# Fused attention and sine MLP: another opening order, the seven-product chain one block later, two of its products swapped

## The chip, the cores and the metric

The kernel runs on one core of a Trainium2 chip. The metric is the device time of one execution in microseconds (us), the median of several runs. The five engines named below are PE (TensorE, matrix products), ACT (ScalarE, table functions and copies), DVE (VectorE, element-wise work), POOL (GpSimd) and SP (SyncE, which here only starts DMAs).

## The reference

Eight batches of eight heads, 576 positions, head size 64. Attention adds a bias that depends on the distance of two positions; its output is reshaped to 4608 tokens of 512 features and goes through a two-layer MLP with a "snake" activation:

```
scores = q @ k.T / 8 + bias_table[bucket(|i - j|)]
attn   = softmax(scores)            # rows of 576
x      = (attn @ v)  as  (4608, 512)
h      = x @ w_in                   # w_in  512 x 2048
g      = h + sin(alpha*h)**2 / (alpha + 1e-9)
out    = g @ w_out                  # w_out 2048 x 512
```

## The kernel before

**Stages.** There is one stage for each batch t = 0..7. A stage has an exp phase and a sin phase, since ACT holds one function table at a time: `tbl` swaps it. In the exp phase PE forms the scores of a head pair and 128 keys (`plan_unit`; kind "A", and small kinds "B", "C" and "X" for the last 64 positions), ACT takes their exponential into `u` (L719), DVE multiplies the band near the diagonal by a table `m2r` or `mhr` of exponentials of the bias (L750, L736), PE multiplies by `v` with a column of ones (`plan_av`), DVE divides by the row sums (L964, L965), and the result is transposed into `xT`, by PE (L1036) and a copy or by a DMA. In the sin phase `plan_moe_in` takes a block b of 512 tokens: for each of 16 slices f of the hidden layer four matmuls `xT,w_in`, then `s` = sin (ACT, L1080), `sq` = s*s (ACT or DVE), and `g` (DVE, L1094). The last stage does two blocks.

**The output product.** Block b is multiplied by `w_out` in stage b+1, wherever PE has room. `plan_mo` does it row by row: four rows of 128 tokens, each 16 matmuls of 512 columns, `w_out,g`. For rows 2 and 3 of the blocks 1 to 6 `plan_chain` takes its place. It is a scheme with seven products in place of eight: two rows by two halves of the hidden layer by two halves of the output columns. Each product is 8 matmuls of 256 columns. DVE makes sums of `g` first (`pre`, into `ss` and into `g`), and the products need four differences of quarters of `w_out`, `wsum`, which `plan_wsum` computes once in stage 1. `take(k, ...)` is what empties product k out of PSUM: a copy to `zz`, or a DVE addition into `outs` (L1367). Two products share a PSUM bank, 0 with 1, 2 with 3, 4 with 5, and 6 has one alone; before, product 4 is `sums(0)` by `wsum[0]` and is emptied twice (`w` and `c22`), and product 5 is `act(1,1)` by `wsum[3]`.

**The order of the work.** Nothing is scheduled at run time. A planner in the kernel (`Plan.run`) places every task on its engine with assumed durations, priorities `pri` and earliest times `nb`, and the program is emitted in that order; on the chip each engine runs its own list in order and waits on semaphores. `QUOTA` and `QUOTA1` bound how many matmuls of the output product may go between the scores of an exp phase (`QUOTA1` for stage 1). `pad` puts filler matmuls on `zz` behind a task of the opening, and `Plan.fill` puts fillers where the planner sees PE idle.

**The opening (stage 0).** The first q and k come as they lie in memory. `plan_tr` transposes a head pair on PE (L562 for the first pair, L568) and a copy puts it into `kT` or `qT` (DVE L551; ACT L549 takes some for batch 1). The tables `m2r` and `mhr` go through DRAM and come back with DMAs on SP's queue. POOL issues `w_in` behind a copy (`tick`, L645) that waits for the last part of `m2r`, and behind `w_in`, on the same queue, the q and k of batch 1 (`nat2`), the four parts of `w_out` (slices f = 0-3, 4-7, 8-11, 12-15) and v of batch 1.

Of the kernel before, what the change touches and what calls it, by code (L numbers as in the profile page):

```python
# [211 lines left out]
WINDOW = 700  # L212
WARM_END = 22.0
QUOTA = 44
QUOTA1 = 32
OFFSET = 0
T_START = 4.0
STEPS = {0: ((1, 1, 1, 1),) * 3, 1: ((3, 1),) * 3}
# [4 lines left out]
T_CL = 24.5  # L223
T_FIRST = (4.75, 5.95)
T_PAIR = ((7.9, 8.5), (9.3, 10.2), (11.6, 12.3))
T_ACT = ()
T_M2 = (13.0, 14.8, 16.0, 16.0)
T_MH = 14.2
T_RST = 25.0
T_V0 = (5.8, 6.4, 8.9, 9.6)  # L230
T_P3 = 7.0
# [7 lines left out]
T_LD = 33.0  # L239

MIX = "nnssss"
CH = ("mo", "mo", "mo", "st")
PIECES = 4
AV_LATE = 9000
# [32 lines left out]
def kernel(  # L277
# [275 lines left out]
    def plan_tr(t, p, kq, pri, nb, deps=()):  # L553

        b, c = Buf("mo"), Cell()

        def mm(e):
            c.v = bank(b).bitcast(F16)
            for i in range(SI):
                x = i * SN  # L560
                if t == 0 and p == 0:
                    nc.tensor.transpose(  # L562
                        out=c.v[:, x : x + SN], in_=natb[:, kq, i], identity=id_sb[0:SN, 0:SN]
                    )
                    continue
                for z in range(2):
                    h = 2 * p - 2 + z if t == 0 else 2 * p + z
                    nc.tensor.transpose(  # L568
                        out=c.v[64 * z : 64 * z + 64, x : x + SN],
                        in_=(nat1 if t == 0 else nat2)[:, kq, h, D * i : D * i + D],  # L570
                        identity=id_sb[0:SN, 0:SN],
                    )

        def cp(e):
            pin = c.v[:, 0:S].rearrange("d (i p) -> d p i", i=SI)

            dst = (kTs, qTs)[kq][t][:, p, :]
            copy_on(e, dst.rearrange("d (p i) -> d p i", i=SI), pin)

        m = plan.add({"PE": 0.4 if t == 0 and p == 0 else 0.5}, mm, deps, pri, nb, new=[b])  # L580
        if t == 0:
            m.pad = (256,) if p else (192,) * (2, 3)[kq]
        eng = {"DVE": 0.75, "ACT": 0.6}
        if t == 0:
            eng = {"ACT": 0.65} if p in T_ACT and kq else {"DVE": 0.75}
        x = plan.add(eng, cp, [m], pri, use=[b])
        if kq:
            return [x], [x]

        def tail(e):  # L590
            for z in range(2):
                r = slice(64 * z, 64 * z + 64)
                k_of(e).tensor_copy(
                    out=kts[t][r, p, r], in_=kTs[t][r, p, 512:S]
                )

        return [x], [plan.add({"POOL": 0.4 if t == 0 else 0.5}, tail, [x], pri + 30)]
# [179 lines left out]
    def plan_att0(g, gates, gate):  # L777

        u, ub, done = Cell(), Buf("u"), {}
        a, b = 2 * g, 2 * g + 1  # L780
        runs = ((a, "A", 0), (a, "A", 1), (a, "A", 2), (a, "C", 0), (a, "A", 3),
                (b, "A", 0), (b, "A", 1), (b, "C", 0), (b, "A", 2), (b, "A", 3))
        exps, head = [], []
        for i, unit in enumerate(runs):
            base = PB + 3200 * g + 300 * i
            x = plan_unit(0, *unit, u, ub, done, gate, base)
            p, kind, _ = unit
            deps = gates + tr[(0, p, 0)][1 if kind == "C" else 0] + tr[(0, p, 1)][0]

            def run(e, i=i, x=x):  # L790
                if i == 0:
                    if g == 0:
                        plan.in_qk, plan.used = True, 0
                        plan.quota = QUOTA
                    u.v = new_u()
                plan.share = (g * len(runs) + i + 1) / (2 * len(runs))
                if g == 1 and i == len(runs) - 1:
                    plan.in_qk = False
                x[2](e)

            d, ends = run_time([unit + (False,)])
            m = plan.add({"PE": d}, run, deps, base, after=head,
                         new=([ub] if i == 0 else []) + [x[0]], use=[] if i == 0 else [ub])
            m.pad = (256,)
            m.offs = ([0.0] if i == 0 else []) + [0.1]
            m.marks = [(x[1], ends[0])]
            head = [m]
            exps += [x[3]]
        for p in (a, b):
            for w in range(2):  # L810
                base = PB + 3200 * g + 600 * ((2, 4)[w] if p == a else 4) + 50 * w
                plan_av(0, [(p, 256 * w), (p, 256 * w + 128)], u, ub, done, base, False)
        return exps
# [66 lines left out]
    def plan_late(base, gate):  # L880

        tb, done = tails[0] = Buf("ut"), {}
        units = [(0, "B", 0), (2, "B", 0), (0, "X", 0)]
        made = [plan_unit(0, *x, None, tb, done, gate, base + 30 * k) for k, x in enumerate(units)]

        def run(e):
            for x in made:
                x[2](e)

        m = plan.add({"PE": 0.78}, run, pe_gate, base, new=[tb] + [x[0] for x in made])  # L890
        m.offs = [0.0, 0.1, 0.32, 0.6]
        m.marks = [(x[1], o) for x, o in zip(made, (0.32, 0.54, 0.78))]
        tail_alone(0, base + 1200)
        return [x[3] for x in made]
# [75 lines left out]
    def plan_av(t, parts, u, ub, done, base, dma):  # L970

        nq = len(parts)
        ab, xb, tb = Buf("av"), Buf("xn"), Buf("h")
        av, xn, tr_ = Cell(), Cell(), Cell()
        prev = []
        p0, q0 = parts[0]
# [187 lines left out]
    def plan_wsum(t, deps):  # L1164
# [9 lines left out]
        )  # L1174
        k, x, y = todo[t]
        for i, d in enumerate(deps):
            r = slice(2 * i, 2 * i + 2)

            def sm(e, k=k, x=x, y=y, r=r):
                nc.vector.tensor_tensor(out=wsum[:, k, r], in0=x[:, r], in1=y[:, r], op=ALU.subtract)  # L1180

            wdone.append(plan.add({"DVE": 0.36}, sm, [d] + wdone[-4:], PB + 9500))

    wdone = []

# [102 lines left out]
    def plan_chain(b, a):  # L1288
# [92 lines left out]
        p = prod(1, lambda: act(0, 1), wq(1, 0), [])  # L1381
        c11 = take(1, (0, 0), (2, 0), [p, x], True)
        yield
        p = prod(2, lambda: sums(1), ws(1), [s2, x] + wdone)
        y = take(2, (1, 1), (2, 0), [p, x], True)
        p = prod(3, lambda: act(1, 0), ws(2), [s3])
        v = take(3, (1, 0), (1, 1), [p, y])
        yield
        p = prod(4, lambda: sums(0), ws(0), [])
        w = take(4, (0, 1), (1, 1), [p, y])  # L1390
        c22 = take(4, (1, 1), (1, 0), [p, v, w])
        p = prod(5, lambda: act(1, 1), ws(3), [])
        take(5, (1, 0), (1, 0), [p, v, c22], last=True)
        yield
        p = prod(6, lambda: sums(2), wq(1, 1), [s4])
        take(6, (0, 1), (0, 1), [p, w, c11], last=True)
# [16 lines left out]
    for t in range(T):  # L1413
# [4 lines left out]
        exps = []  # L1418
        for p in range(NP - 1) if t == 0 else ():
            for kq in range(2):  # L1420
                tr[(0, p + 1, kq)] = plan_tr(0, p + 1, kq, (150, 650, 5)[p], T_PAIR[p][kq])
        if t == 0:
            for g in range(2):
                exps += plan_att0(g, pe_gate, gate)
        else:
            exps += plan_att(t, pe_gate, gate)
            if t == 1:
                for i in range(4):
                    plan_wsum(i, exps[3 * i + 1 : 3 * i + 4] + exps[3 * i + 3 : 3 * i + 4])
            if t == 1:  # L1430
                exps += plan_late(PB + LATE, gate)
        if t == 0:
# [21 lines left out]
            sins += s_  # L1454
        pe_gate = [m]
        if t < T - 1:
            if t:
                rows, ch = iter((0, 1)), plan_chain(t, 2)
                for x in MIX:
                    if x == "n":  # L1460
# [3 lines left out]
            else:  # L1464
                for a in range(4):
                    plan_mo(t, a)
        else:
            for b in (t, t + 1):
                for a in (0, 2):
# [32 lines left out]
```

## Time and profile before

| what | value |
|---|---|
| median of 3 runs | 369.23 us (368.93 to 372.27) |
| the profiled execution, its own time | 368.74 us |
| its span (first to last instruction) | 366.8 us, so 1.9 us lie around it |
| granted TensorE clock | 1.0 |
| PE busy | 356.8 us, 97% of the span |
| ACT busy | 312.3 us, 85% |
| DVE busy | 309.2 us, 84% |
| POOL busy | 92.0 us, 25% |

All times in rows are us from the span's start. A row of the timeline has the start, the length, the engine, the line, the operation, its names and shapes, how many instructions were merged, and in brackets the idle time ahead of it with what ended that. Matmuls overlap: a row of n matmuls lasts n-1 intervals and the length of one. So a "busy" PE can still have lost some tenths of a microsecond at a gap, since the next matmul needs its full length again before its result is there.

### The profile page before, as it was taken

What the parts mean: (1) busy time and instruction counts of PE and PEld (TensorE: products, weight loads), DVE (VectorE), ACT (ScalarE), POOL (GpSimd) and SP (SyncE); (2) the same over time, 40 slices, a digit from 0 to 9 for tenths busy, and PEclk for the clock granted to TensorE, in tenths of its full rate; (3) what the DMA queues carried; (4) which work ended last, traced back from release to release, by engine and by line L of the source; (5) the groups of instructions that cost most, each with busy time, mean ns of one, the idle gap of its engine ahead of it and who ended that gap; (6) DMA issues with size and microseconds to landing.
All of it is one profiled execution on the core that took longest, in us unless ns stands there. A gap on an engine that the chain in (4) does not pass through costs nothing.

```text
span 366.8 us, 9604 instructions
## 1 busy us (share of the span) xinstructions
PE 356.8 (97%) x3808; PEld 218.9 (60%) x3808; DVE 309.2 (84%) x748; ACT 312.3 (85%) x430; POOL 92.0 (25%) x133
## 2 busy tenths in 40 slices
PE   7889999999999999999999999999999999999996
PEld 3464545644475446885684457545776468456685
DVE  4797979878977998699978998798869997899982
ACT  3988999889897999799988999799979997996711
POOL 7477350064000830047000900082006000000000
PEclk9999999999999999999999999999999999999999
DMA  9999999599724996299917992599529421001122
GB/s 170 198 172 204 200 162 148 115 97 122 111 53 102 127 150 108 78 143 113 152 52 153 87 173 55 134 125 128 104 79 163 35 79 50 15 2 57 44 74 87
DMA packets 150269, 40.53 MB, mean 110 GB/s; under 512 B 137208, under 2 KB 145616, under 8 KB 150224
## 3 DMA queue, kind: packets, MB, share of 16 engines
q0 software_dynamic: 96032, 17.67, 59.6%
q1 hardware_dynamic: 54016, 22.16, 25.9%
q8 instruction: 30, 0.49, 0.6%
q14 instruction: 15, 0.12, 0.1%
q10 hardware_dynamic: 176, 0.09, 0.1%
HBM read 37.73 MB, written 16.56 MB: 148 GB/s over the span
## 4 chain that ended last, share of the span: by engine, by line
PE 83%; ACT 10%; DVE 4%; issue 2%; ACTq 0%
PE pb L469 82%; ACT u L719 8%; ACT s L1080 1%; DVE outs L1367 1%; DVE u L750 1%; ACT sq L1087 1%; PE pb L1036 1%; PE pb L568 0%; ACT kT L549 0%; DVE nat L763 0%; ACT qT L549 0%; DVE xn L965 0%; PE pb L562 0%; DVE qT L551 0%; DVE zz L551 0%
## 5 line engine op out<-in xcount | busy, mean ns | idle before, releaser
L719 ACT ACTIVATE u<-pb 128x1024 f16<-128x1024 f32 (+1 forms) x146 | 136.8, 1022 | 10.3 <-PE pb L469 9.6
L469 PE MATMUL pb<-xT,w_in 128*128 128x512 f16 (+4 forms) x704 | 128.1, 340 | 0.0
L1094 DVE SCALAR_TENSOR_TENSOR g<-sq,inv_a,pb 128x512 f16<-128x512 f16 x144 | 101.1, 743 | 3.7 <-ACT sq L1087 2.0
L1080 ACT ACTIVATE s<-pb,alphaT 128x512 f16<-128x512 f32 x144 | 92.8, 693 | 12.8 <-PE pb L469 12.0
L469 PEld LDWEIGHTS <-w_in 128*128 128x128 f16 x704 | 64.7, 98 | 56.1 <-issue 0.3
L469 PE MATMUL pb<-w_out,g 128*128 128x512 f16 (+1 forms) x416 | 81.7, 339 | 0.5 <-DVE zz L551 0.5
L469 PEld LDWEIGHTS <-g 128*128 128x128 f16 x552 | 51.4, 98 | 37.6 <-issue 7.2
L750 DVE TENSOR_TENSOR u<-u,m2r 128x512 f16<-128x512 f16 (+1 forms) x128 | 61.6, 489 | 11.4 <-ACT u L719 8.6
L469 PEld LDWEIGHTS <-u 128*128 128x128 f16 x1280 | 56.0, 97 | 9.1 <-issue 3.8
L414 POOL COPY kt<-kT 64x256 f16<-64x256 f16 x12 | 5.2, 432 | 172.4 <-DMA kT<-staged_k 142.9
L1087 ACT ACTIVATE sq<-s 128x512 f16<-128x512 f16 x69 | 43.4, 639 | 2.0 <-DVE g L1094 1.1
L469 PE MATMUL pb<-qT,kT 64*128 64x64 f16 (+1 forms) x512 | 42.7, 285 | 1.8 <-DVE qT L551 0.6
L469 PE MATMUL pb<-v,u 128*128 128x65 f16 x1024 | 44.1, 193 | 0.3 <-DVE u L750 0.2
L1089 DVE TENSOR_TENSOR sq<-s 128x512 f16<-128x512 f16 x75 | 31.7, 432 | 10.8 <-ACT s L1080 10.1
L965 DVE TENSOR_TENSOR xn<-pb,rd 128x256 f16<-128x256 f32 (+2 forms) x59 | 28.5, 483 | 2.0
L469 PEld LDWEIGHTS <-kT 64*128 64x128 f16 x512 | 16.1, 94 | 22.4 <-issue 15.4
L469 PE MATMUL pb<-vh,u 128*128 128x130 f16 x128 | 28.2, 221 | 0.1
L419 POOL DMA_DIRECT2D v<-in_v_dram x28 | 24.8, 896 | 3.9 <-DMA nat<-in_k_dram 2.3
L1403 ACT ACT_TABLE_LOAD x15 | 19.2, 1283 | 0.3
L469 PE MATMUL pb<-wsum,g 128*128 128x256 f16 (+1 forms) x136 | 18.6, 266 | 0.9
L719 ACT ACTIVATE nat<-pb 128x1024 f16<-128x1024 f32 (+1 forms) x24 | 17.7, 817 | 0.0
L1367 DVE TENSOR_TENSOR outs<-pb,outs 128x256 f32<-128x256 f32 x30 | 12.6, 421 | 5.3 <-PE pb L469 4.7
(97 smaller groups left out, 303.0 us busy)
## 6 DMA issues: line engine op xcount, KB each, us to landing
out_dram<-outs SPq DMA_DIRECT2D x28, 256.0 KB, 2.9
v<-in_v_dram POOLq DMA_DIRECT2D x28, 128.0 KB, 4.5
staged_k<-in_k_dram POOLq DMA_DIRECT2D x6, 576.0 KB, 8.6
staged_q<-in_q_dram POOLq DMA_DIRECT2D x6, 576.0 KB, 12.4
w_in<-in_moe_w_in_dram POOLq DMA_DIRECT2D x4, 512.0 KB, 8.4
w_out<-in_moe_w_out_dram POOLq DMA_DIRECT2D x4, 512.0 KB, 14.7
out_dram<-outs SPq DMA_DIRECT2D x15, 128.0 KB, 1.7
w_out<-in_v_dram SPq DMA_DIRECT2D x6, 128.0 KB, 4.3
```

The source lines that it names most:

```text
L414: nc.gpsimd.tensor_copy(out=kts[t % 2][r, :, r], in_=kTs[t % 2][r, :, 512:S])
L419: nc.gpsimd.dma_start(out=vs[t % 2][:, c, :, 0:D], in_=vp[128 * c : 128 * c + 128],)
L469: nc.tensor.matmul(out=out, lhsT=lhsT, rhs=rhs, start=start, stop=stop, skip_group_check=go_on)
L719: nc.scalar.activation(out=o, in_=x, func=AF.Exp, scale=0.125)
L750: nc.vector.tensor_tensor(out=io, in0=io, in1=m2[:, 2 * p : 2 * p + 2, x0 : x0 + hi - lo], op=ALU.mult)
L965: nc.vector.tensor_tensor(out=xn[:, 0:n].rearrange("p c (z d) -> p c z d", z=2), in0=x[:, :, :, 0:D], in1=r.unsqueeze(3).to_broadcast([128 ...
L1080: nc.scalar.activation(out=s16.v, in_=h.v, func=AF.Sin, scale=alphaT[:, f : f + 1])
L1087: nc.scalar.activation(out=sq.v, in_=s16.v, func=AF.Square)
L1089: k_of(e).tensor_tensor(out=sq.v, in0=s16.v, in1=s16.v, op=ALU.mult)
L1094: nc.vector.scalar_tensor_tensor(out=gcell[b].v[:, f, :], in0=sq.v, scalar=inv_a[:, f : f + 1], in1=h.v, op0=ALU.mult, op1=ALU.add,)
L1367: nc.vector.tensor_tensor(out=put(i, j), in0=at(k), in1=put(*x), op=ALU.add)
L1403: nc.scalar.preload_act_table_set(name)
```

## The change

- **The chain one block later** (`FIRST = 2`): block 1 has all four rows by `plan_mo`. What chain 1 issued for the staging of batch 3 (POOL DMAs `staged_k`, `staged_q`) is planned in stage 1.
- **`wsum`**: two of the four differences in stage 1 and two in stage 2, in 32 pieces of 256 elements a row in place of 16 of 512.
- **Products 4 and 5 of the chain change places**: `act(1,1)` by `wsum[3]` is first, in the first half of the bank, and `sums(0)` by `wsum[0]`, emptied twice, is second. Product 2 no longer lists the copy of product 0 as a dependency.
- **`QUOTA1`** 44 in place of 32.
- **The opening**: no `pad` behind the transposes of pairs 1 to 3 nor behind the scores; other priorities and earliest times for the transposes (`T_TP`) and the bands (`T_M2`, `T_MH`); the last pair's `attn @ v` may take any bank (`P_ST`).
- Two assumed durations of the planner (`plan_tr`'s copy on ACT, the late scores of batch 0).

In the built program PE has 16 fillers of 256 columns fewer and 5 of 192 more; 32 more matmuls `w_out,g` of 512 columns, and 56 fewer of 256 columns. DVE has 750 instructions before and 742 after, ACT 436 and 438, POOL and SP as many as before.

```diff
-QUOTA1 = 32
+QUOTA1 = 44
...
 T_PAIR = ((7.9, 8.5), (9.3, 10.2), (11.6, 12.3))
+T_TP = ((450, 450), (650, 650), (5, 5))
 T_ACT = ()
-T_M2 = (13.0, 14.8, 16.0, 16.0)
-T_MH = 14.2
+P_ST = 3
+T_M2 = (14.85, 15.9, 17.0, 17.0)
+T_MH = 15.9
...
 MIX = "nnssss"
+SUMS = {1: (0, 1), 2: (2, 3)}
+FIRST = 2
...
         if t == 0:
-            m.pad = (256,) if p else (192,) * (2, 3)[kq]
-        eng = {"DVE": 0.75, "ACT": 0.6}
+            m.pad = () if p else (192,) * (2, 3)[kq]
+        eng = {"DVE": 0.75, "ACT": 0.53}
...
-            m.pad = (256,)
             m.offs = ([0.0] if i == 0 else []) + [0.1]
...
-        m = plan.add({"PE": 0.78}, run, pe_gate, base, new=[tb] + [x[0] for x in made])
+        m = plan.add({"PE": 0.5}, run, pe_gate, base, new=[tb] + [x[0] for x in made])
...
-        ab, xb, tb = Buf("av"), Buf("xn"), Buf("h")
+        ab, xb, tb = Buf("st" if t == 0 and parts[0][0] >= P_ST else "av"), Buf("xn"), Buf("h")
...
-            r = slice(2 * i, 2 * i + 2)
+            r = slice(i, i + 1)
...
-            wdone.append(plan.add({"DVE": 0.36}, sm, [d] + wdone[-4:], PB + 9500))
+            wdone.append(plan.add({"DVE": 0.218}, sm, [d] + wdone[-8:], PB + 9500))
...
-        p = prod(2, lambda: sums(1), ws(1), [s2, x] + wdone)
+        p = prod(2, lambda: sums(1), ws(1), [s2] + wdone)
...
-        p = prod(4, lambda: sums(0), ws(0), [])
-        w = take(4, (0, 1), (1, 1), [p, y])
-        c22 = take(4, (1, 1), (1, 0), [p, v, w])
-        p = prod(5, lambda: act(1, 1), ws(3), [])
-        take(5, (1, 0), (1, 0), [p, v, c22], last=True)
+        prod(4, lambda: act(1, 1), ws(3), [])
+        p = prod(5, lambda: sums(0), ws(0), [])
+        w = take(5, (0, 1), (1, 1), [p, y])
+        c22 = take(5, (1, 1), (1, 0), [p, v, w])
+        take(4, (1, 0), (1, 0), [p, v, c22], last=True)
...
-                tr[(0, p + 1, kq)] = plan_tr(0, p + 1, kq, (150, 650, 5)[p], T_PAIR[p][kq])
+                tr[(0, p + 1, kq)] = plan_tr(0, p + 1, kq, T_TP[p][kq], T_PAIR[p][kq])
...
-            if t == 1:
-                for i in range(4):
-                    plan_wsum(i, exps[3 * i + 1 : 3 * i + 4] + exps[3 * i + 3 : 3 * i + 4])
+            for i in SUMS.get(t, ()):
+                plan_wsum(i, exps[2:18:2])
...
-            if t:
+            if t >= FIRST:
...
                 for a in range(4):
                     plan_mo(t, a)
+                if to_stage:
+                    n_, x = to_stage.pop()
+                    plan.add({"POOL": 4.5}, lambda e, n_=n_: stage_kq(n_), [x], PB + 9600)
```

## The prediction

> **What bounds the kernel now.** I read the page first, then the busy time by stage, then the chain of waits and PE's timeline around each gap. The stages below run from one stage's first scores to the next one's.
>
> ```profile
> PE 356.8 (97%) x3808; PEld 218.9 (60%) x3808; DVE 309.2 (84%) x748; ACT 312.3 (85%) x430; POOL 92.0 (25%) x133
> ...
> 25.00:47.00 22.00, 21.48 (x279) 12.02 (x275) 19.10 (x40) 20.69 (x36) 13.54 (x28) 1.00 1.22 204
> 47.00:89.60 42.60, 42.60 (x402) 21.85 (x400) 35.69 (x87) 39.08 (x55) 14.85 (x14) 1.00 1.37 125
> 89.60:129.20 39.60, 38.83 (x406) 22.37 (x405) 33.96 (x87) 35.81 (x48) 8.32 (x11) 1.00 0.78 105
> 129.20:168.30 39.10, 38.85 (x471) 27.96 (x470) 33.93 (x86) 35.92 (x48) 9.02 (x11) 1.00 1.02 117
> 168.30:207.70 39.40, 39.15 (x409) 22.86 (x408) 34.41 (x87) 35.96 (x48) 10.00 (x12) 1.00 1.02 114
> ```
>
> The first number after the length is PE's busy time. From 25 us on PE is without work for 0.52 us, then 0.00, 0.77, 0.25 and 0.25 us a stage, while DVE has over 5 us and ACT over 3 us free in each stage. So the time is PE's work plus its few gaps, and an edit counts by the PE work that it adds, the gaps that it closes, and whether PE comes to work earlier at the start. Its gaps in the later stages are all like this one, seen in the chain of waits and then in PE's timeline:
>
> ```profile
> 188.59 0.42 DVE outs L1367
> 189.01 0.20 DVE nat L763
> 189.21 0.34 DVE outs L1367
> 189.56 0.04 issue
> 189.60 1.58 PE pb L469 x13
> ```
>
> ```profile
> 188.28 0.27 PE L469 MATMUL pb<-wsum,g 128*128 128x256 f16 x1
> ...
> 189.05 0.41 PE L469 MATMUL pb<-v,u 128*128 128x65 f16 x8
> 189.60 0.92 PE L469 MATMUL pb<-wsum,g 128*128 128x256 f16 x7
> ```
>
> Product 5 has issued one matmul (188.28) and waits with the other seven until DVE has read product 4 twice out of the same bank.
>
> **Products 4 and 5 swapped.** The gap is 189.60 - (189.05 + 0.41) = 0.14 us. More is lost than the gap: behind it a matmul needs its whole 0.27 us again, while within a row of n the next one follows after (0.92 - 0.27)/6 = 0.11 us. So a gap costs itself plus 0.27 - 0.11 = 0.16, here 0.30 us. In the new order `act(1,1)` by `wsum[3]` fills the first half of the bank, `sums(0)` by `wsum[0]` the second, and only then does DVE read; product 6 has a bank of its own. PE then has nothing to wait for at this place, and what DVE now does later (two additions, 0.42 us each) is needed by stores and by product 6's addition, not by PE. The built order puts the division of the last pair (`rd`, `xn`), which PE's transposes need, ahead of the second addition, so it is not late. The chain remains in stages 3 to 7: 5 x 0.30 = -1.50 us. Bounds: 0, if the burst of three additions makes another bank late, and 5 x 0.30.
>
> **Block 1 without the chain.** PE work first: 7 x 8 = 56 matmuls of 256 columns at 0.11 us go, 32 of 512 columns come. Their interval is (2.97 - 0.38)/12 = 0.216 us, by the row of 13 matmuls at 46.42 (quoted with the opening below) and the mean of one, 379 ns. 32 x 0.216 - 56 x 0.11 = 6.91 - 6.16 = +0.75 us on PE, which has no cover there.
>
> ```profile
> L469 PE MATMUL pb<-w_out,g x25: 376/379/390, 46.4 to 54.8; 128*128 128x512 f16 x25
> ...
> 97.61 2.18 PE L469 MATMUL pb<-w_out,g 128*128 128x512 f16 x14
> 100.30 0.27 PE L469 MATMUL pb<-w_out,g 128*128 128x256 f16 x1 [0.51 <-DVE zz L551]
> ...
> 102.59 0.60 PE L469 MATMUL pb<-w_out,g 128*128 128x256 f16 x4
> 103.30 0.22 PE L469 MATMUL pb<-vh,u 128*128 128x130 f16 x1
> ```
>
> Then the gaps of stage 2, 0.77 us against 0.25 in the later ones. The wait for DVE's copy of product 0 to `zz` is 0.51 + 0.16 = 0.67 us, and this stage has the wait of 0.30 described above too; both go with the chain: -0.97. The gap at 103.30 (0.11 us, 0.27 with the refill) waits for DVE's `xn`, which is late behind the chain's sums; I do not count it, since `wsum` pieces now stand there. Stage 2 in sum: 0.75 - 0.97 = -0.22 us, between -0.49 and +0.75.
>
> The `wsum` pieces are unseen at 256 elements a row. The nearest row has 0.42 us for 512, so a piece costs between 0.21 and 0.42 us (I take 0.21, in proportion), and 16 of them 3.4 to 6.7 us of DVE in stage 1 (which loses 16 x 0.42 = 6.7) and in stage 2 (which loses the chain's 16 sums and its additions). Stage 2 has 39.60 - 33.96 = 5.6 us of DVE free: 0. Without that cover it would show as `xn` late for PE. The staging of batch 3 stands at the same place of POOL's list, behind the loads of v: 0.
>
> ```profile
> L1180 DVE TENSOR_TENSOR wsum<-w_out x3: 420/420/420, 53.4 to 54.3; 128x512 f16<-128x512 f16 x3
> ```
>
> **The opening: what it could bring.** DVE and ACT before:
>
> ```profile
> 14.90 0.42 DVE L750 TENSOR_TENSOR u<-u,m2r 128x512 f16<-128x512 f16 x1 [1.70 <-DMA m2r<-e_dram]
> 15.25 0.75 DVE L551 COPY kT<-pb 128x576 f16<-128x576 f16 x1
> 15.91 0.75 DVE L551 COPY qT<-pb 128x576 f16<-128x576 f16 x1
> 16.58 1.25 DVE L750 TENSOR_TENSOR u<-u,m2r 128x768 f16<-128x768 f16 x2
> ...
> 19.35 3.35 ACT L719 ACTIVATE u<-pb 128x1024 f16<-128x1024 f32 x4 [0.49 <-PE pb L469]
> 23.31 1.02 ACT L719 ACTIVATE u<-pb 128x1024 f16<-128x1024 f32 x1 [0.61 <-PE pb L469]
> 24.23 0.38 ACT L549 ACTIVATE xT<-pb 128x256 f16<-128x256 f16 x1
> ```
>
> The last pair's two copies now go into the 1.70 us in which DVE waits for `m2r`: the bands behind them start 16.58 - 15.25 = 1.33 us earlier. ACT's waits for PE (0.49 and 0.61) and the copy of 0.38 leave the row of exponentials: 1.48 us. So the first block could come 1.3 to 1.5 us earlier; the removed fillers lie where PE is ahead of ACT and are worth nothing by themselves.
>
> **The opening: what stops it.** PE's work of block 0 needs data that one DMA queue brings:
>
> ```profile
> L455 POOL DMA_DIRECT2D w_out<-in_moe_w_out_dram x4: 755/765/770, 29.2 to 31.5; - x4
> ...
> DMA to landing us min/median/max: 11.6/14.7/17.4
> ```
>
> ```profile
> 18.26 0.42 POOL L645 COPY tick<-m2r 1x1 f16<-1x1 f16 x1 [0.84 <-DMA m2r<-e_dram]
> 18.62 2.90 POOL L450 DMA_DIRECT2D w_in<-in_moe_w_in_dram  x4
> ```
>
> ```profile
> 46.42 2.97 PE L469 MATMUL pb<-w_out,g 128*128 128x512 f16 x13
> 49.32 1.00 PE L469 MATMUL pb<-qT,kT 64*128 64x512 f16 x6
> ```
>
> The last part of `w_out` lands at 31.5 + 17.4 = 48.9 us. It is issued 17 us before that, so the queue sets the time and not the issue; the queue's work starts with `w_in` at 18.62, behind a copy that waits for `m2r`, and nothing of this is changed. PE's 13th product (slice 12, the first that needs that part) starts at 46.42 + 12 x 0.216 = 49.01 us: only 0.1 us behind the landing. In the new order all that stands ahead of the 13th product is the same work (64 matmuls of block 0, the transposes of batch 1, the late scores of batch 0, 12 products). However early PE gets there, it waits until 48.9: of 1.3 to 1.5 us it keeps 0.1. What is late next is the exp phase of stage 1: before its first scores the new order has 17 products and the old one 13. They start at 48.9 + 5 x 0.216 + 0.1 = 50.1 in place of 49.32, so ACT, which took its first of them at 49.81, starts at about 50.5. It gets back the copy of `xT`, now on DVE:
>
> ```profile
> 49.81 3.77 ACT L719 ACTIVATE u<-pb 128x1024 f16<-128x1024 f32 x4
> 53.44 0.42 ACT L549 ACTIVATE xT<-pb 128x256 f16<-128x256 f16 x1
> 54.05 2.85 ACT L719 ACTIVATE u<-pb 128x1024 f16<-128x1024 f32 x3 [0.19 <-PE pb L469]
> ...
> 67.73 2.21 ACT L719 ACTIVATE nat<-pb 128x1024 f16<-128x1024 f32 x3
> ```
>
> 54.05 - 53.44 = 0.61. The phase would end at 69.94 + 0.7 - 0.6, as before. PE has 37 products in it where it had 44 (despite the larger quota, since four stand ahead of it), and enters the sin phase with 54 done in place of 57. If it enters at the same time, it is 3 x 0.216 = 0.65 us behind; if ACT's waits for PE shrink with the lighter load, it is level or 0.1 ahead. I take +0.3, near the middle; bounds -1.4 (no wall) and +0.65.
>
> **The sum**, against the profiled execution's 368.74 us: -1.50 - 0.22 + 0.3 = -1.42, or 367.3. The undisturbed runs shown, 368.93 and 369.23, lie 0.34 above the profiled one in the mean, so a median is forecast at **367.6 us**. Its own range has stage 2 at -0.49 with the wall's 0.1 kept, 367.0, and stage 2 at +0.75 with stage 1 at +0.65, 369.0.
>
> **The rivals.**
> 1. *The opening is kept.* The queue's end moves with the rest, or the 13th product waits less. For it: the landing is one execution's, and 0.1 us of slack says only that PE came just behind it. Against it: 17 us from issue to landing. It puts -1.4 in the place of +0.3: 367.6 - 1.7 = 365.9 us, and 365.6 if the gap at 103.30 goes too.
> 2. *The swap brings nothing.* The three additions run behind product 5, and the next `attn @ v` or product finds its bank held, so that 0.30 us a stage is lost at another place. For it: the DVE row of additions is as long as before. Against: product 6 and the transposes do not read that bank. 367.6 + 1.5 = 369.1 us, no change.
> 3. *PE's clock falls in the opening*, which ends on the slower side. The first row below has 8 matmuls of 512 and 2 of 192 columns, 4480 in all, in 3.72 us: 0.83 ns a column, against 0.216/512 = 0.42 later. So PE does run at half rate in this kernel, at the start, though the granted clock reads 1.00 throughout.
>
> ```profile
> 1.27 3.72 PE L469 MATMUL pb<-zz 128*128 128x512 f16 x10 [1.27 <-DVE zz L520]
> ```
>
> The fillers may be what ends that and holds it off. Until 17 us half rate is hidden, since ACT needs about 0.9 us for a unit of scores and PE 0.43 at half rate. From 17 to 25 us it is not: sixteen parts of `attn @ v` at 0.29 (188.39 to 188.69 in PE's timeline is one) and seven units of scores at 0.22 are 6.2 us of work, which would take 12.4 in 8 us. That is 4.4 us late, less the 1.4 that the wall would have eaten: 367.6 + 3.0 = 370.6 us. It decides from the point where the half rate outlasts 19 us or so.
>
> ```profile
> 188.39 0.22 PE L469 MATMUL pb<-vh,u 128*128 128x130 f16 x1
> ...
> 188.69 0.22 PE L469 MATMUL pb<-vh,u 128*128 128x130 f16 x1
> ```
>
> The Trainium skill bears on this: "TensorE: Matmul & The Clock Gate", part 1, has the array at half rate until about 3.4 us of sustained work and again after an idle window of that length, and part 4 says that transposes do not count as work in the same way. The row above agrees with the first; no run here yet shows the rest. By that page the 36 transposes and few scores between 8 and 13 us might let the clock fall, and the time would be this rival's if it stayed down past 17 us; I see no gap of 3.4 us in the new order.
>
> **How the numbers follow.** The forecast 0.55, rival 1 0.18, rival 2 0.19, rival 3 0.05, something unseen 0.03. The range 365.1 to 369.7 leaves out rival 3 and the edges. A measurement of this kernel tells about 1% (3.7 us) from no change. Faster by more than that, below 365.5, is under half of rival 1, whose size by itself is uncertain by half a microsecond, and a part of the unseen: 0.09. Slower by more, above 372.9, is rival 3's upper part: 0.03. Within 1%: 0.88.
>
> **What would show it.** Right: in PE's list a wait of about 1 us for the DMA of `w_out` at its 13th product, near 48.9 us, with the first scores of stage 1 near 50.1; no gap ahead of the chain's products in stages 3 to 7 and a stage of 39.1 us in place of 39.4 there; no wait for `zz` in stage 2. Wrong: first scores of stage 1 before 49 us (rival 1), stages 3 to 7 still 39.4 us long (rival 2), `attn @ v` parts of over 0.4 us each in the first 25 us (rival 3).

## The result and the profile after

The changed kernel takes 367.5 us (median of 17 executions, 366.85 to 369.6), the kernel before 369.2 us beside it (17 executions, 368.68 to 372.27). The ratio is 0.9948, interval 0.9929 to 0.9967: 1.7 us less, which is within 1%. The forecast was 367.6. Its terms did not all come out that way: that the total came so near is partly luck, since errors of both signs cancelled.

Two executions of the changed kernel were profiled. The first took 369.33 us (span 367.5), the second 366.91 (span 365.1). They differ in the opening and then run alike, 2.4 us apart; the section on the hardware takes that up. The comparison here is between the second one and the profiled execution of before (368.74, span 366.8). The page of the second one begins:

```profile
span 365.1 us, 9530 instructions
...
PE 355.2 (97%) x3773; PEld 216.1 (59%) x3773; DVE 306.1 (84%) x740; ACT 313.0 (86%) x432; POOL 92.8 (25%) x133
```

PE is still the bound. The 1.70 us between the spans can be placed by the rows in which ACT loads its other table, since they mark where a phase ends. These are ACT's table loads in the timeline, before first and then after: the end of stage 0's exponentials, the end of its sin phase, the ends of the sin phases of stages 2 and 3, and the last load.

```profile
27.27 1.28 ACT L1403 ACT_TABLE_LOAD   x1
46.39 1.28 ACT L1403 ACT_TABLE_LOAD   x1
...
128.77 1.28 ACT L1403 ACT_TABLE_LOAD   x1
...
167.90 1.28 ACT L1403 ACT_TABLE_LOAD   x1
...
307.75 1.28 ACT L1403 ACT_TABLE_LOAD   x1
```

```profile
26.20 1.28 ACT L1406 ACT_TABLE_LOAD   x1
46.28 1.28 ACT L1406 ACT_TABLE_LOAD   x1
...
127.92 1.28 ACT L1406 ACT_TABLE_LOAD   x1
...
167.39 1.28 ACT L1406 ACT_TABLE_LOAD   x1
...
306.32 1.28 ACT L1406 ACT_TABLE_LOAD   x1
```

| stretch | before, us | after, us | difference | forecast |
|---|---|---|---|---|
| start to the end of the first exponentials | 27.27 | 26.20 | -1.07 | -1.3 to -1.5 |
| to the end of the first sin phase | 19.12 | 20.08 | +0.96 | given back at the wall |
| stages 1 and 2 | 82.38 | 81.64 | -0.74 | all three rows together +0.08 |
| stage 3 | 39.13 | 39.47 | +0.34 | -0.30 |
| stages 4 to 7, to the last load | 139.85 | 138.93 | -0.92 | with the next row -1.20 |
| the rest | 59.05 | 58.78 | -0.27 | |

The first two rows compare one execution of each kernel, and the opening scatters by as much from one execution to the next (run 3 below). How far PE is ahead of ACT also differs from one table load to another, so the rows of stages 1 to 3 are taken up again by PE's own list in the section on why.

**The place of the swap.** PE's timeline in stage 4, the place that the prediction shows of before at 188.28 to 189.60:

```profile
187.76 0.27 PE L473 MATMUL pb<-wsum,ss 128*128 128x256 f16 x1
...
188.53 0.41 PE L473 MATMUL pb<-v,u 128*128 128x65 f16 x8
188.78 0.93 PE L473 MATMUL pb<-wsum,ss 128*128 128x256 f16 x7
```

From the last row of `v,u` to the seven matmuls behind it are 188.78 - 188.53 = 0.25 us; before, 189.60 - 189.05 = 0.55. PE no longer stops between the two products of a bank, and 0.30 us went.

The prediction's reading that the gaps in the later stages "are all like this one" is not right. Of the 0.25 us a stage, 0.14 is this wait; the other 0.10 is a wait of PE's scores for ACT's `u` (at 183.37 before). It is still there in the changed kernel's stages 4 to 7 (at 182.86, for one).

**The wait for zz is still there.** The waits of PE in the changed kernel from 46.4 to 306 us (in total, times, longest), and the two places in its timeline:

```profile
PE pb L473 <- DVE zz L555: 0.5, 1, 0.5
PE pb L473 <- ACT u L723: 0.4, 1, 0.4
```

```profile
67.36 0.41 PE L473 MATMUL pb<-qT,kT 64*128 64x64 f16 x16 [0.40 <-ACT u L723]
...
142.33 0.27 PE L473 MATMUL pb<-w_out,g 128*128 128x256 f16 x1 [0.52 <-DVE zz L555]
```

This view leaves out waits as short as the 0.14 for `outs`; in PE's timeline none of those is left. The wait for `zz` is the wait that stood in stage 2 before, at 100.30. It has moved by one stage, to the stage that now has the first chain.

### The profile page after: what moved, and what is told of

It is laid out like the page before. It is cut to its first block, busy times and chain, and to the rows that moved or that the text cites. A ratio compares the mean times of both kernels' runs of the same rounds, so it can differ in the third digit from the quotient of the medians.

```text
span 367.5 us, 9530 instructions
## 1 busy us (share of the span) xinstructions
PE 360.0 (98%) x3773; PEld 217.6 (59%) x3773; DVE 305.9 (83%) x740; ACT 313.6 (85%) x432; POOL 91.7 (25%) x133
## 4 chain that ended last, share of the span: by engine, by line
PE 90%; ACT 6%; DVE 2%; issue 1%; DVEq 0%; ACTq 0%
PE pb L473 88%; ACT u L723 5%; PE pb L572 1%; DVE g L1097 1%; PE pb L1039 1%; ACT sq L1090 0%; PE pb L566 0%; DVE sq L1092 0%; ACT xT L553 0%; DVE qT L555 0%; ACT qT L553 0%; DVE kT L555 0%; ACT s L1083 0%; ACT kT L553 0%; DVE zz L555 0%
## 5 line engine op out<-in xcount | busy, mean ns | idle before, releaser
L473 PE MATMUL pb<-w_out,g 128*128 128x512 f16 (+1 forms) x432 | 88.4, 344 | 0.5 <-DVE zz L555 0.5
L473 PE MATMUL pb<-qT,kT 64*128 64x64 f16 (+1 forms) x512 | 44.4, 294 | 1.3 <-ACT u L723 0.4
L553 ACT ACTIVATE u<-pb 128x256 f32<-128x256 f32 x12 | 4.6, 386 | 14.7 <-PE pb L473 14.7
L406 POOL DMA_DIRECT2D staged_q<-in_q_dram x6 | 16.7, 2786 | 0.0
```

Of the source, the lines that this page charges most:

```text
L406: nc.gpsimd.dma_start(out=dst.ap()[t].rearrange("s (h d) -> s h d", h=H), in_=src[t].rearrange("h s d -> s h d"),)
L473: nc.tensor.matmul(out=out, lhsT=lhsT, rhs=rhs, start=start, stop=stop, skip_group_check=go_on)
```

## The experiments

Each kernel ran in 12 executions (6 where that is said), next to the kernel before on the same chip. The kernel before had medians of 368.96 (35 executions), 369.10 (29) and 369.22 (29) in the three sets.

**1. The changed kernel once more.**

> The changed kernel unaltered, for a second profile. The first one was of an execution at 369.33 us in which PE's matmuls of the opening took about twice as long until 20.7 us; the median was 367.5. Theory (wall): an execution near 367.2 us, its opening matmuls at full rate, its 13th output product waiting 0.5 to 1.5 us for the last quarter of w_out near 49 us, stages 3 to 7 of 39.05 us. Rival (opening kept): no such wait, and the 13th product at 47.5 to 48.5 us. Rival (clock): the opening is slow here too, since the removed fillers no longer wake PE, and about 369 us.

367.19 us (366.51 to 369.28), ratio 0.9952, interval 0.9931 to 0.9974. The result is repeated. The second profile above is this run's.

**2. The swap undone.** In the changed kernel, products 4 and 5 stand as they stood before:

```diff
-prod(4, lambda: act(1, 1), ws(3), [])
-p = prod(5, lambda: sums(0), ws(0), [])
-w = take(5, (0, 1), (1, 1), [p, y])
+p = prod(4, lambda: sums(0), ws(0), [])
+w = take(4, (0, 1), (1, 1), [p, y])
...
+p = prod(5, lambda: act(1, 1), ws(3), [])
```

> The changed kernel with products 4 and 5 of the chain in the order of before. Theory: 0.30 us in each of the 5 stages that have a chain, so 1.5 us slower than the changed kernel, about 368.8 us, and the wait of 0.14 us for DVE's additions is back in each. Rival (the burst of additions costs as much elsewhere): no slower.

369.01 us (367.91 to 370.99), ratio 0.9992, interval 0.9967 to 1.0018: all that the change brings is gone. In PE's timeline of this kernel the stop is back at its place:

```profile
190.76 0.41 PE L473 MATMUL pb<-v,u 128*128 128x65 f16 x8
191.32 0.92 PE L473 MATMUL pb<-wsum,g 128*128 128x256 f16 x7
```

191.32 - 190.76 = 0.56 us, as before. From the median the swap is worth 1.8 us, where five stages of 0.30 make 1.5. This profile's opening was slow (its first table load stands at 28.13), but behind it the two profiles can be compared stage by stage: from the table load at the end of stage 2 on, each of the stages 3 to 6 is 0.29 to 0.31 us longer than with the swap and the rest 0.26, 1.47 in all.

**3. The old opening.** The changed kernel with the fillers, priorities, earliest times and bank of the old opening (`pad=(256,)`, `T_M2`, `T_MH`, `T_TP`, `P_ST` and the two assumed durations undone).

> The changed kernel with the opening of before (fillers, priorities, earliest times, banks). Theory (wall): the opening is worth nothing, 367.2 to 367.9 us, within 0.3 of the changed kernel beside it. Rival (opening kept): 1.3 us slower than the changed kernel, 368.5 to 369. Rival (clock): fewer slow executions than the changed kernel, median 0.3 or more below it.

367.04 us (366.31 to 370.42), ratio 0.9956, interval 0.9929 to 0.9984. The new opening brings nothing that can be seen in the medians.

The traces agree. The kernels of before and of runs 3, 5 and 6 have the same order of work in the opening; their profiles have the first table load at 27.27, 26.65, 26.77 and 26.28 us, and ACT's first sine at 30.55, 29.99, 30.30 and 29.64. With the new opening (runs 1, 4, 8 and 10) the load is at 26.20, 26.67, 26.89 and 26.28, the first sine at 30.01, 30.45, 30.70 and 30.09. So the profile of before was the slowest of its kind, and most of the -1.07 in the table is scatter.

**4. The chain undone.** The changed kernel with the chain from block 1 on, `wsum` in 16 pieces in stage 1, and `QUOTA1 = 32`:

```diff
-QUOTA1 = 44
+QUOTA1 = 32
-            if t >= FIRST:
+            if t:
```

> The changed kernel with the chain from block 1 on, as before (wsum and the smaller quota of stage 1 too). Theory as in the prediction, corrected for the swap: 0.75 us of PE work less, the wait of 0.67 us for the copy to zz back in stage 2 beside nothing in stage 3: 0.1 us faster to 0.2 slower. Rival (the wait for zz belongs to the first chain, whichever block it has, as the profile after suggests, where it stands in stage 3): only the PE work counts, 0.75 us faster than the changed kernel, 366.5 to 366.8 us.

367.87 us (366.15 to 369.54), ratio 0.9955, interval 0.9927 to 0.9984; span 365.1, the same as the second profile's. No difference is shown in the medians. The stages do differ: from the table load at the end of stage 1 to the one at the end of stage 3 this kernel takes 78.42 us (88.96 to 167.38) against 79.16 (88.23 to 167.39), so by these loads leaving the chain out of block 1 costs 0.74 there, near the 0.75 of PE work in the prediction. The spans are equal because this execution was as much later at the end of stage 1 (88.96 against 88.23); 0.44 of that is the opening's (46.72 against 46.28). In its timeline PE waits for `zz` in stage 2, and in no later one:

```profile
103.30 0.27 PE L471 MATMUL pb<-w_out,g 128*128 128x256 f16 x1 [0.51 <-DVE zz L553]
```

So that wait belongs to the first chain, whichever block that is.

**5. The swap alone.** The kernel before with the swap and product 2's shorter list of dependencies, nothing else.

> The kernel before with products 4 and 5 of the chain swapped (and product 2's dependency on the copy of product 0 dropped); the chain still begins with block 1, the opening is the old one. Theory: the swap is the whole of what the change gained, 0.30 us in each of six stages here, so 1.8 us: a stage of 39.1 us from the second on, stage 2 included, and 368.96 - 1.8 = 367.2 us, level with the whole change (367.2). Rival: the later chain carries a part (what stage 2 gains by it, -0.22 by the prediction): then stage 2 still has its 0.67 for the copy zz and the time is 367.4 or more. Rival: the swap pays only with the later chain's room on DVE: over 368.

367.31 us (366.58 to 370.59), span 365.0; ratio 0.9977, interval 0.9950 to 1.0005. The median and the span are the whole change's. The interval reaches to 1 because four executions lie above 370. The swap alone is enough for the result, though here it acts in six stages: 6 x 0.30 = 1.80 us, the difference of the spans (366.8 and 365.0). In the changed kernel it acts in five, and the other parts of the change come to some tenths together. The wait for `zz` is still there (0.52 at 100.37). This profile also shows a wait for the last part of `w_out` at the 13th product, which the section on why takes up:

```profile
49.22 0.38 PE L469 MATMUL pb<-w_out,g 128*128 128x512 f16 x1 [0.30 <-DMA w_out<-in_moe_w_out_dram]
```

**6. The swap, and a dependency for product 1.** The planner did not know that product 1 waits for the copy of product 0 out of the same bank. Here it is told so:

```diff
-p = prod(1, lambda: act(0, 1), wq(1, 0), [])
+p = prod(1, lambda: act(0, 1), wq(1, 0), [x])
```

> As the kernel before with the swap alone, and product 1 of the chain lists the copy of product 0 (zz) as a dependency, so that the planner puts other PE work between them where the copy is late. Theory: the 0.67 us that the first chain loses at this place (gap 0.51 and refill 0.16) goes, and nothing comes in its place: 367.2 - 0.67 = 366.5 us. Rival: what the planner moves ahead leaves PE short at another gap, and the time stays 367.2 or rises; the later stages, which have no wait there, may then show one.

365.80 us (6 executions, 364.86 to 367.84), span 363.0; ratio 0.9925, interval 0.9900 to 0.9950. ACT's table loads at both ends of stage 2, of the swap alone and then with the dependency:

```profile
89.03 1.28 ACT L1403 ACT_TABLE_LOAD   x1
...
128.22 1.28 ACT L1403 ACT_TABLE_LOAD   x1
...
284.61 1.28 ACT L1403 ACT_TABLE_LOAD   x1
```

```profile
88.23 1.28 ACT L1403 ACT_TABLE_LOAD   x1
...
126.74 1.28 ACT L1403 ACT_TABLE_LOAD   x1
...
282.68 1.28 ACT L1403 ACT_TABLE_LOAD   x1
```

Stage 2 goes from 39.19 to 38.51 us: -0.68, where gap and refill were put at 0.67. The match is in part chance: the wait of 0.11 for `xn` in that stage (at 103.37) went as well, and one of 0.20 for ACT's `u` came (at 99.46). The four stages behind it go from 156.39 to 155.94, so 0.11 less each; that was not expected. It is the wait of 0.10 for ACT's `u` in each of the stages 3 to 7: PE's timeline of the swap alone has it, and this one has not. Together that is 0.68 + 0.45 = 1.13 us. Of the 2.0 by which the spans differ, another 0.67 lies in the opening (end of the first sin phase at 45.47 against 46.14), which has the same order of work in both.

**7. The same kernel again.**

> The swap alone with the dependency of product 1, once more beside the changed kernel with the same dependency. Theory: 365.8 again, and 0.3 below the other, which has 0.75 us more of PE work in stage 2 (no chain for block 1) and an opening that gains some tenths. Rival: the two are level, since the first chain's cost in stage 2 eats what its seven products save: both 366.

366.09 us (365.05 to 369.67), ratio 0.9923, interval 0.9893 to 0.9954. This is the fastest version: 1.1 to 1.4 us below the changed kernel's 367.2 by the medians, though the intervals of the ratios overlap.

**8. The same dependency in the changed kernel.**

> The changed kernel, and product 1 of the chain lists the copy of product 0 (zz) as a dependency for the planner. With the swap alone this addition brought 1.5 us (365.8 in place of 367.3): 0.67 in the first chain's stage and about 0.11 in each of the later ones, in which PE's last idle tenth went. Theory: the changed kernel has the same wait, in stage 3 (gap 0.52), and the same tenths in four later stages: 367.2 - 0.67 - 0.4 = 366.1 us, with no gap for zz in stage 3. Rival: the gain came from another place of the old opening or of block 1's chain, which this kernel does not have: 367.2, or 0.67 less at most.

374.79 us (6 executions, 374.45 to 377.23), ratio 1.0154, interval 1.0118 to 1.0189. Every theory missed by 7 us or more. In PE's timeline there is no wait for `zz` in stage 3, and the stage is 0.75 shorter (table loads at 128.77 and 167.49, 38.72 against 39.47). But PE has other waits, here by kind from 46.9 us to the end, and then two of them at both ends of stage 5's exp phase:

```profile
PE pb L473 <- DVE outs L1370: 3.4, 7, 0.5
PE pb L1039 <- DVE xn L968: 1.5, 4, 0.4
```

```profile
206.38 1.25 PE L473 MATMUL pb<-wsum,g 128*128 128x256 f16 x10 [0.52 <-DVE outs L1370]
...
229.81 0.34 PE L1039 MATMUL pb<-id_sb,xn 128*128 128x128 f16 x3 [0.37 <-DVE xn L968]
```

Stage 5, between the table loads at 206.50 and 246.62, takes 40.12 us against 39.03. The first of the two waits is again two products of one bank, now 2 and 3: told of one such wait, the planner put another order together and met the next one, which it does not know of either. The larger part of the loss lies behind the last load at 309.42: 373.3 - 309.42 = 63.88 us against 58.78. That is the last sin phase and what runs behind it, and more products are left over for it: from the first scores of stage 7 on, PE's timeline has 32 products of 512 columns in place of 20. Stage 3 has 12 fewer. Why the planner leaves them over was not followed further.

**9. Few fillers at the start.** The changed kernel with `WARM0 = 2` in place of 8.

> The changed kernel with 2 of the 8 filler matmuls at the start of PE's list. In its first profile the changed kernel ran its matmuls at half rate until 20.7 us and took 2.4 us more than in its second profile. Theory: half rate lasts until PE has worked without a pause for some us, and the fillers at the start end it in most executions: with fewer of them most executions are slow ones, about 369.6 us, with rows of attn @ v of 0.65 us for 8 matmuls in place of 0.40 up to 20 us. Rival: which rate the opening gets does not hang on these fillers: 367.2 in most executions, about one in eight at 369.5.

368.96 us (368.48 to 370.16), ratio 1.0000, interval 0.9986 to 1.0014. Not one execution is as short as the changed kernel's median, so the fillers at the start do count. In PE's timeline there is a pause of 2.20 us at the start, and the matmuls keep half rate until 20.3 us. That the pause is the reason isn't shown: the first profile of the changed kernel has no such pause and the same half rate.

```profile
4.83 0.66 PE L566 MATMUL pb<-id_sb,natx 96*128 96x96 f16 x6 [2.20 <-DVE natx L483]
...
19.85 0.64 PE L473 MATMUL pb<-v,u 128*128 128x65 f16 x8
...
20.39 0.41 PE L473 MATMUL pb<-v,u 128*128 128x65 f16 x8
```

**10. The last quarter of w_out not loaded.** Zeros stand in its place, so the output leaves that part out.

```diff
-        for fh in range(4):
+        for fh in range(3):
+    nc.vector.memset(w_out16[:, 12:16, :], 0.0)
```

> The changed kernel without the load of the last quarter of w_out (slices 12-15); zeros are written in its place, so the output leaves that part out. By the prediction the 13th output product of block 0 waits for this load at 48.9 us, and 1.3 us that the new opening gains are lost to the wait: without the load stage 1 starts earlier, 366.0 to 366.3 us. By the theory since: there is no wait (in the second profile the load lands at 48.28 and PE comes to the 13th product at 48.73), the gain is lost before, between the last exponential and the first sine: first scores of stage 1 at 49.9 as before, 367.2 us, no difference.

367.09 us (366.42 to 369.15), ratio 0.9947, interval 0.9926 to 0.9968, and the first scores of stage 1 are at 49.96, as with the load (49.90). In the changed kernel the wall of the prediction costs nothing.

**11. The fillers of the opening put back.** The changed kernel with `pad = (256,)` behind the transposes of pairs 1 to 3 and behind the scores.

> The changed kernel with the removed fillers of 256 columns put back behind the transposes of pairs 1 to 3 and behind the scores of the opening. Question: do the removed fillers decide whether the opening runs at half rate? Theory: no, the ones at the start of PE's list do (with 2 of those 8 every execution took 368.5 or more); the share of executions at 369 and above stays about one in seven, and the median is the changed kernel's, 367.2, within 0.3. Rival: they do, and no execution lies above 368.5, with a median of 366.9 to 367.1.

367.93 us (366.58 to 372.37), ratio 0.9964, interval 0.9932 to 0.9996. Three of twelve executions lie above 370.9. The removed fillers did not hold the slow openings off. Whether they make them dearer is not settled by three executions.

**12. The last pair's attn @ v in its old bank.** The changed kernel with `P_ST` undone.

> The changed kernel with the last pair's attn @ v in its old bank kind (P_ST undone), the rest of the new opening kept. In the second profile of the changed kernel the exponentials end 0.45 us earlier than with the old opening, and the first sine starts at the same 30.0: the last pair's attn @ v, division, transposes and copies set that. Theory: the bank is what lets this last chain run at all as early as in the old opening; undone, the first sine comes 0.3 to 0.6 later and the time is 367.5 to 367.8. Rival: the bank is not what the last chain waits for: 367.2 and the first sine at 30.0.

367.62 us (366.83 to 368.59), ratio 0.9951, interval 0.9934 to 0.9969. The median is where the theory had it, but this ratio is not told apart from the first run's 0.9952. In the profile the first sine starts at 30.86, 4.24 us behind the table load at 26.62; with any bank it starts at 30.01, 3.81 behind 26.20. That is 0.43 us for the bank. The 4.24 is of one execution; with any bank the same stretch takes 3.77 to 3.81 in all eight profiles.

## Why the prediction was right, and where it was not

**The swap: right, and in its size.** That a gap costs itself plus 0.16 us, here 0.30, is what the traces show (0.55 to 0.25 us at the place; stages 4 to 7 and the rest -1.19 against -1.20 forecast), and undoing it takes away all of the gain, 1.47 us from stage 3 on. Rival 2, that the wait comes back at another place, is refuted for this order. In run 8, in another order, waits of products that share a bank did appear at another place.

**Block 1 without the chain: the step failed by which the wait for DVE's copy of product 0 to `zz` goes with the chain (0.67 of the -0.97).** It left stage 2 and came back in stage 3 in full size (0.51 before, 0.52 after), so stage 3 is longer, by 0.34 from ACT's loads and 0.09 from PE's first scores, in place of 0.30 shorter. The prediction took the wait as belonging to block 1; run 4 shows that it belongs to the first chain, and run 6 that an unplanned dependency between the two halves of a bank causes it: listed, the wait is gone. In the stages behind the first chain product 1 comes later by itself (in stage 4 the copy is done at 179.13, and seven matmuls of product 1 start at 180.69).

**The opening: the result near nothing was right, the reason was wrong.** Two steps failed: "nothing of this is changed", with "however early PE gets there, it waits until 48.9", the wall at the last quarter of `w_out`; and ahead of it "the first block could come 1.3 to 1.5 us earlier". In the second profile, POOL's issues with their DMAs, and then PE's rows ahead of stage 1:

```profile
L459 POOL DMA_DIRECT2D w_out<-in_moe_w_out_dram x4: 755/765/770, 27.5 to 29.7; - x4
...
DMA to landing us min/median/max: 13.0/15.9/18.5
```

```profile
45.31 0.38 PE L473 MATMUL pb<-w_out,g 128*128 128x512 f16 x1
...
46.35 3.62 PE L473 MATMUL pb<-w_out,g 128*128 128x512 f16 x16
...
49.90 0.82 PE L473 MATMUL pb<-qT,kT 64*128 64x512 f16 x6
```

The last part lands at 29.7 + 18.5 = 48.2 us. One product stands at 45.31, so the 13th is the twelfth of the next row, at 46.35 + 11 x 0.216 = 48.73, and the row has no gap (15 x 0.216 + 0.38 = 3.62). Run 10 shows the same from the other side. The queue was not fixed: it starts earlier when the opening is earlier. But PE was not early either. The forecast of 50.1 for the first scores is met (49.90), for PE's own work: 17 products.

The margin is small, though, 0.5 us in this profile, and the wall is real in others: PE waits for that DMA 0.30 us in run 5, 0.16 and 0.31 in runs 6 and 7, and 0.64 in run 9. So the prediction had the right wait, and took a moment that moves with the opening for a fixed one.

The first block was not 1.3 to 1.5 us earlier either. By the profiles listed under run 3, ACT's first sine is at 29.64 to 30.55 us with the old opening and at 30.01 to 30.70 with the new one. What the new order gains in the exponentials it gives back between the last exponential and the first sine: from the table load to the first sine it takes 3.8 us, the old one 3.3 to 3.5. PE, ACT and DVE of the second profile there, and then two rows of before:

```profile
25.16 1.02 ACT L723 ACTIVATE u<-pb 128x1024 f16<-128x1024 f32 x1 [0.85 <-PE pb L473]
...
26.50 0.41 DVE L754 TENSOR_TENSOR u<-u,m2r 128x512 f16<-128x512 f16 x1
...
28.27 0.42 DVE L968 TENSOR_TENSOR xn<-pb,rd 128x256 f16<-128x256 f32 x1
...
29.60 1.02 PE L473 MATMUL pb<-xT,w_in 128*128 128x512 f16 x4 [0.26 <-ACT xT L553]
```

```profile
27.10 0.41 DVE L750 TENSOR_TENSOR u<-u,m2r 128x512 f16<-128x512 f16 x1
...
29.50 1.01 PE L469 MATMUL pb<-xT,w_in 128*128 128x512 f16 x3
```

The forecast had ACT's waits for PE gone from the exponentials; ACT still waits 0.85 us ahead of the last one. The last band is multiplied 0.60 us earlier than before (26.50 against 27.10), and the run of `w_in` begins 0.10 later: behind the band come the last parts of `attn @ v`, the division at 28.27, the transposes and ACT's copy, one after the other, and PE has a wait of 0.26 for that copy. PE has done two more matmuls of `w_in` by then, which is 2 x 0.216 = 0.43 us, so it is 0.33 ahead. From there to 46.35 its waits add up to 0.44 us, and to 0.47 before, so nothing is given back or won. At the first scores of stage 1 it is 0.28 ahead: 49.90 against 49.32, with four products more (0.86 us).

**Stages 1 to 3 by PE's own list.** PE's first scores of the stages 2, 3 and 4, before and then in the second profile:

```profile
89.60 0.82 PE L469 MATMUL pb<-qT,kT 64*128 64x512 f16 x6
...
129.45 0.82 PE L469 MATMUL pb<-qT,kT 64*128 64x512 f16 x6
...
169.16 0.82 PE L469 MATMUL pb<-qT,kT 64*128 64x512 f16 x6
```

```profile
88.79 0.82 PE L473 MATMUL pb<-qT,kT 64*128 64x512 f16 x6
...
128.85 0.82 PE L473 MATMUL pb<-qT,kT 64*128 64x512 f16 x6
...
168.65 0.82 PE L473 MATMUL pb<-qT,kT 64*128 64x512 f16 x6
```

Counted in PE's timeline, 77 products by `w_out` lie ahead of the first of these rows before and 73 after, so 4 x 0.216 = 0.86 us of work is still to come there. At the other two rows the output product has come equally far in both kernels.

| stretch, by PE's first scores | measured | forecast |
|---|---|---|
| opening and stage 1 | 88.79 + 0.86 - 89.60 = +0.05 | +0.30 |
| stage 2 | 39.20 - 39.85 = -0.65 | -0.22 |
| stage 3 | 39.80 - 39.71 = +0.09 | -0.30 |
| the rest | 196.45 - 197.64 = -1.19 | -1.20 |

In stage 1 PE loses the 0.28 that it was ahead, and 0.05 more; its only longer wait there is the 0.40 at 67.36. In stage 2 it has no wait at all, where before it had three: 0.51 for `zz`, 0.11 for `xn` at 103.30 and 0.14 for `outs`. The prediction did not count the one for `xn`; with it the stage comes to -0.49, its own lower bound, and 0.16 more stays unexplained. So a gain of 0.43 and one of 0.25 that were not forecast cover the 0.39 by which stage 3 missed. Had the wait for `zz` gone as forecast, the kernel would have come out 0.7 to 1 us below the forecast.

**The `wsum` pieces** took 0.28 us each, between the two bounds (0.21 taken), and no `xn` was late for them in stage 2, as forecast. Two of them, in a view of groups that ends at 56 us:

```profile
L1183 DVE TENSOR_TENSOR wsum<-w_out 128x256 f16<-128x256 f16 x2 | 0.6, 284 | 0.0
```

**Rival 3** got 0.05 as a loss in every execution. As a loss in some executions it is real, and its price is near the one worked out (2.4 us between the two profiles, against 3.0). The step "the fillers may be what ends that and holds it off" is right for those at the start (run 9) and not for those that the change removes (run 11).

## What to carry to other kernels

When two results share a PSUM bank, fill both halves before the first is read, and tell the planner of every wait between them; here one swapped pair was worth 0.30 us a stage and one listed dependency 0.68 once and 0.11 in each later stage, in one order. Compare more than one execution before calling a difference in the opening a gain: the same order of work ended its first phase anywhere from 26.28 to 27.27 us. When a wait disappears from the place where a change was made, look for it at the next place of the same kind before counting it as a gain. Try such a dependency in the very order that will run: the same line saved 1.2 to 1.5 us in one order and cost 7.6 in another.

## What the runs showed of the hardware

**The same kernel, two rates in the opening.** PE's rows of `attn @ v` in the first profile of the changed kernel:

```profile
20.21 0.65 PE L473 MATMUL pb<-v,u 128*128 128x65 f16 x8
...
20.76 0.42 PE L473 MATMUL pb<-v,u 128*128 128x65 f16 x8
```

Eight matmuls took 0.65 us up to 20.7 us and 0.42 from there on, while in the second profile such rows take 0.40 to 0.41 from 16.6 us on (but for one, at 22.43, with a wait in it). The granted clock is given as 1.00 in both. The end of the exponentials is at 28.69 in one and 26.20 in the other, and everything behind it is 2.4 us apart, so the opening is the whole difference, and its rate is what the two rows show to differ. With the old opening it costs more, by one profile of each kind: of the two profiles of the kernel in runs 6 and 7, the slower one reaches its first table load at 30.93 in place of 26.28, and the spans are 367.7 and 363.0. So the new opening seems to be worth something after all, but only in an execution whose opening is at half rate. Which executions these are, the times alone don't tell; 4 of 29 of the changed kernel lie at 369.2 or above.

**The rate fell behind a pause of 1.72 us.** In the profile of run 2 the opening was at full rate until PE had to wait for a band:

```profile
16.49 0.41 PE L473 MATMUL pb<-v,u 128*128 128x65 f16 x8
...
18.77 0.46 PE L473 MATMUL pb<-v,u 128*128 128x65 f16 x5 [1.72 <-DVE u L754]
...
19.13 0.65 PE L473 MATMUL pb<-v,u 128*128 128x65 f16 x8
...
21.96 0.52 PE L473 MATMUL pb<-v,u 128*128 128x65 f16 x8
```

The five matmuls behind the pause are already at half rate (they start 0.054 us apart, where those before it start 0.029 apart), and the rate rises again within the last row, at 22.14 us.

The Trainium skill, "TensorE: Matmul & The Clock Gate", part 1, gives about 3.4 us of idleness for the fall and about 3.4 us of sustained work for the return, watched in a window that runs freely, so that one kernel can differ from run to run. That two executions differ agrees with the traces, and so does the return in the profile of run 2: from 18.77 to 22.14 is 3.4 us. The other lengths do not agree: there the longest pause before the fall was 1.72 us, and the first profile of the changed kernel and run 9 kept half rate from 1.26 to 20.7 and from 4.83 to 20.3 us, with no wait over 0.4 us. Part 4 of that page has transposes not counting as work like other matmuls. Those of the pairs 1 to 3 lie in that stretch, up to 16.4 us in run 9, which would fit. In run 7 it fits less well: there they last until 19.1 us, and full rate is back in the row at 21.12. No run here takes them away, so it isn't shown.
